# The last pair of the first network: down product by seven products of halves, with weight sums made in the same pair

## The chip, the core and the metric

The kernel runs on one core of a Trainium2 chip. The core has TensorE (PE, matmuls into PSUM), VectorE (DVE), ScalarE (ACT), GpSimd (POOL) and SyncE (SP). Each has an instruction queue of its own that runs in order. SP and ACT issue the DMAs of this kernel, and 16 DMA engines carry them. The metric is the device time in microseconds (us), the median of several executions; one more execution was recorded by the hardware profiler.

## The reference

All data are float32. Attention in chunks of 64 tokens gives x (4608 x 512); then come two networks, each with an up product, a gate, and a down product.

```python
x = ...                                        # attention, 4608 x 512
xn = x / sqrt(mean(x * x) + 1e-6) * rms_g
g, val = xn @ w_gate, xn @ w_val               # 512 -> 1536 each
y = (g * sigmoid(g) * val) @ w_out             # 1536 -> 512, the first network
h = y @ w_in2                                  # 512 -> 2048
out = (h * clip(h + 3, 0, 6) / 6) @ w_out2     # 2048 -> 512, the second network
```

The inputs of attention are drawn as normal numbers of a spread near 0.38 for q and k and 0.1 for v.

## The kernel before

A matrix is kept as two parts of reduced float32 (F32R), a high one and the rest, and a product takes three matmuls: high by high, low weight by high, high weight by low. Tokens go in nine blocks of 512. Blocks 0 to 2 of the first network are computed plainly; blocks 3 to 8 go in three pairs (the loop over `p`, L1359).

In a pair, the up matrix works by seven products of halves in place of eight (`Operands` makes the sums of the weights once, early, and keeps them in DRAM as `ops`; `x_ops` makes those of the inputs). There are 84 products of six matmuls each (`product`), in groups of 14: in a group the products 1, 1, 4, 3, 4, 3, 5, 6, 5, 6, 2, 7, 2, 7 follow each other, numbered by the table at L1394 on, each with a half `m` of 128 columns. Products 1 and 2 gather in PSUM banks 2 and 3 of this pair (`bank(0, m)`), 4, 6 and 7 in banks 6 and 7, 3 and 5 in banks 4 and 5. Behind each product ACT copies or applies silu out of PSUM, VectorE adds or multiplies out of PSUM (L1357), POOL multiplies the two branches. The activations are left in tiles `ge` (one big one) and `gu`.

The down matrix of the pair is computed plainly (`mm_down_a`): 24 items, one for each of 12 slices of 128 rows and each of the two blocks, 12 matmuls an item. `split_wp` makes the two parts of an activation (ACT the high one, POOL the rest), two items ahead. The weights `w_out` in two parts were kept in DRAM as `keep_out` by `keep_w`.

What sets the order is written out by hand. `Loads` (L456) has a list of all weight tiles in the order of use; each tile used up issues the next load on SP's queue, six tiles ahead of use; a load's tile comes from a pool of 36 buffers. A `tick` (L1194) stands behind every second up product and every down item; a pair has 66 ticks. At a tick the functions run that `at(t, ...)` put there: units of attention (in the first two pairs alone), the second network's weights (`Stash`: raw weights loaded by ACT's queue, turned on ACT, VectorE and POOL, and stored to `stash_in` and `stash_out` in 24 ticks each, eight times, until the end of this pair), norms, and the sums of inputs. In the last pair's down half SP also loads block 0 of y (`load_x2`), fourteen of the second network's down weights (`fetch_out`) and the first six tiles of its stream (`Stream`, in the attention's buffers q, k, qT, kT, p, v).

The second network's pairs do their down product by seven products of halves already: `product_down` (L1578), 56 steps of six matmuls; `feed` splits an activation four steps ahead, on VectorE. Its weight sums were made by `turn_out` during the second network's block 0.

The lines that the prediction speaks of:

```python
def product(bank, op, x, first=True, last=True): ...   # six matmuls, L1029
yb = [(*bk[0], *bk[1]), (*bk[4], *bk[0])]               # L1452, down items
t = gt(f0, 0)
vec(t, t, bank(0, 1), ALU.mult)                         # product 2, half 1: empties bank 0's second half
```

## Time and profile before

| | |
|---|---|
| median of 3 runs | 1655.03 us (1654.75 to 1655.18) |
| the profiled execution | 1654.2 us |
| its span in the trace | 1652.4 us |
| TensorE busy | 1640.0 us, 99% |
| VectorE, ACT, POOL busy | 1030.2, 846.1, 453.4 us (62%, 51%, 27%) |
| moved by DMA | 375.08 MB, mean 227 GB/s |

The span begins with the first instruction of the program and ends with the last; the profiled execution's time has 1.8 us around it. Times inside the trace are counted from the span's start. An engine that is busy for less of the span isn't therefore without effect: TensorE waits for it wherever it is late with one instruction.

### The profile page before, as it was taken

The numbers are of one execution on the slowest core, as the hardware profiler recorded it, in microseconds if no ns is written. First come the engines' busy times: TensorE is split into PE (matmuls) and PEld (weight loads), VectorE is DVE, ScalarE is ACT, GpSimd is POOL, SyncE is SP. The second block draws the span as 40 slices with busy tenths as digits, with TensorE's granted clock in tenths as the row PEclk, the third lists the DMA queues.
The fourth block names the chain that finished last, engine by engine and source line by source line (L and its number), as shares of the span: only waits on it lengthen the run. The fifth ranks groups of instructions, "written<-read, shape, count | busy, mean of one in ns | idle before, by whom it ended". The sixth has DMA issues, their size and how long they took to land.

```text
span 1652.4 us, 26451 instructions
## 1 busy us (share of the span) xinstructions
PE 1640.0 (99%) x9920; PEld 1350.1 (82%) x9920; DVE 1030.2 (62%) x1533; ACT 846.1 (51%) x1409; POOL 453.4 (27%) x333
## 2 busy tenths in 40 slices
PE   8999999999999999999999999999999999999999
PEld 7788887888888888888888888888888888888887
DVE  6887566655575755748334388358746764875475
ACT  6885445355464454635444334455545544654553
POOL 1002434322226432354226522141024003301310
PEclk8999999999999999999999999999999999999999
DMA  9914776738976688865979676767876796788666
GB/s 303 277 44 100 212 208 204 224 135 248 314 263 226 208 286 289 274 210 199 346 241 327 260 268 205 228 192 249 219 216 219 214 243 197 224 222 231 196 194 163
DMA packets 336098, 375.08 MB, mean 227 GB/s; under 512 B 184289, under 2 KB 260065, under 8 KB 335841
## 3 DMA queue, kind: packets, MB, share of 16 engines
q1 hardware_dynamic: 266080, 302.32, 59.7%
q10 hardware_dynamic: 69888, 71.06, 12.6%
q8 instruction: 79, 1.29, 0.3%
q14 instruction: 51, 0.41, 0.1%
HBM read 292.55 MB, written 80.74 MB: 226 GB/s over the span
## 4 chain that ended last, share of the span: by engine, by line
PE 95%; DVE 2%; DMA 1%; ACT 1%; issue 0%; SPq 0%; POOL 0%; DVEq 0%; POOLq 0%
PE PS L1029 39%; PE PS L1581 18%; PE PS L1018 13%; PE PS L1043 6%; PE PS L1044 6%; PE PS L1046 6%; PE PS L923 1%; PE PS L850 1%; DMA wo<-ops 1%; PE PS L832 1%; PE PS L1051 1%; PE PS L1055 1%; PE PS L1052 1%; PE PS L1783 1%; PE PS L794 0%
## 5 line engine op out<-in xcount | busy, mean ns | idle before, releaser
L1029 PE MATMUL PS<-xu,wo 128*128 128x512 f32 x1512 | 350.2, 391 | 0.5 <-DVE xu L1243 0.5
L1029 PEld LDWEIGHTS PS<-xu,wo 128*128 128x128 f32 x1512 | 282.1, 188 | 59.8 <-DVE xu L1243 0.9
L1029 PE MATMUL PS<-xo,wq 128*128 128x512 f32 x1344 | 305.3, 389 | 0.0
L1581 PE MATMUL PS<-gs,wq 128*128 128x512 f32 x1296 | 295.3, 389 | 0.0
L1029 PEld LDWEIGHTS PS<-xo,wq 128*128 128x128 f32 x1344 | 252.3, 188 | 52.4
L1581 PEld LDWEIGHTS PS<-gs,wq 128*128 128x128 f32 x1296 | 242.9, 188 | 51.7 <-DVE gs L1575 1.2
L1018 PE MATMUL PS<-XH,w 128*128 128x512 f32 x576 | 147.9, 399 | 2.7 <-ACT XH L656 1.9
L1018 PEld LDWEIGHTS PS<-XH,w 128*128 128x128 f32 x576 | 107.1, 190 | 26.4 <-ACT XH L656 2.2
L1043 PE MATMUL PS<-gs,wd 128*128 128x512 f32 x288 | 113.2, 393 | 0.0
L1044 PE MATMUL PS<-gs,wd 128*128 128x512 f32 x288 | 112.2, 389 | 0.0
L1074 POOL TENSOR_TENSOR al<-sg,ah 128x512 fp32r<-128x512 f32 x40 | 55.8, 1396 | 154.6 <-ACT ah L1072 150.3
L1353 POOL TENSOR_TENSOR gs<-gu,gs 128x512 fp32r<-128x512 f32 x60 | 84.3, 1423 | 45.9 <-ACT gs L1352 39.9
L1357 DVE TENSOR_TENSOR gu<-gu,PS 128x512 f32<-128x512 f32 x60 | 41.1, 686 | 83.0 <-ACT gu L1439 45.8
L1649 POOL TENSOR_TENSOR gt<-gx 128x512 f32<-128x512 f32 x8 | 10.3, 1290 | 296.5 <-DVE gx L1646 296.5
L1575 DVE TENSOR_TENSOR gs<-gu,gs 128x512 fp32r<-128x512 f32 x88 | 67.9, 791 | 32.0 <-ACT gs L1574 31.7
L1574 ACT CAST gs<-gt 128x512 fp32r<-128x512 f32 x96 | 58.1, 623 | 43.9 <-DVE gt L1718 33.5
L1512 DVE SCALAR_TENSOR_TENSOR gu<-gu,PS 128x512 f32<-128x512 f32 x48 | 32.8, 684 | 72.9 <-ACT gu L1509 72.9
L1018 PE MATMUL PS<-XL,w 128*128 128x512 f32 x288 | 77.9, 393 | 0.0
L1046 PE MATMUL PS<-gs,wd 128*128 128x512 f32 x288 | 77.0, 389 | 0.0
L1072 ACT CAST ah<-sg 128x512 fp32r<-128x512 f32 x52 | 32.4, 624 | 84.7 <-DVE sg L1330 53.2
L1574 ACT CAST gs<-gu 128x512 fp32r<-128x512 f32 x96 | 57.4, 621 | 25.2 <-DVE gs L1575 17.7
L1649 POOL TENSOR_TENSOR gt<-gu 128x512 f32<-128x512 f32 x24 | 32.5, 1355 | 129.0 <-DVE gu L1646 124.9
(249 smaller groups left out, 2823.8 us busy)
## 6 DMA issues: line engine op xcount, KB each, us to landing
wq<-stash_in SPq DMA_DIRECT2D x128, 512.0 KB
wo<-ops SPq DMA_DIRECT2D x126, 512.0 KB
wq<-sums_out SPq DMA_DIRECT2D x64, 512.0 KB
wq<-stash_out SPq DMA_DIRECT2D x48, 512.0 KB
wd<-keep_out SPq DMA_DIRECT2D x36, 512.0 KB
yd<-yst SPq DMA_DIRECT2D x18, 512.0 KB
ops<-w ACTq DMA_DIRECT2D x36, 256.0 KB
v<-in_v_dram SPq DMA_DIRECT2D x32, 256.0 KB
```

What stands on the lines that cost most here:

```text
L1018: nc.tensor.matmul(ps, w(wi, c), xs[c][xi], start=(i == 0), stop=(i == n - 1))
L1029: nc.tensor.matmul(PS[:, bank, :], op[:, wi, c * 128:(c + 1) * 128], x[xi][:, c, :], start=first and i == 0, stop=last and i == 5, skip_gr ...
L1043: nc.tensor.matmul(ps, wm[0], a[0], start=first, stop=False)
L1044: nc.tensor.matmul(ps, wm[1], a[0], start=False, stop=False)
L1046: nc.tensor.matmul(PS[:, banks[m], :], w[:, 0, m * 128:(m + 1) * 128], a[1], start=False, stop=last)
L1074: nc.gpsimd.tensor_tensor(lo, t, hi.bitcast(F32), op=ALU.subtract)
L1353: e.tensor_tensor(w[:, 1, :], t, w[:, 0, :].bitcast(F32), op=ALU.subtract)
L1357: nc.vector.tensor_tensor(o, x, y, op=op)
L1574: nc.scalar.copy(w[:, 0, :], x)
L1575: e.tensor_tensor(w[:, 1, :], x, w[:, 0, :].bitcast(F32), op=ALU.subtract)
L1581: nc.tensor.matmul(PS[:, banks[m], :], op[:, wi, m * 128:(m + 1) * 128], x[xi], start=first and (wi, xi) == (0, 0), stop=False, skip_group ...
L1649: nc.gpsimd.tensor_tensor(slot(i, "t"), slot(i, "12"), slot(i, "11"), op=ALU.subtract)
```

## The change

For the last pair alone the 24 down items become 42 steps of `product_down`: seven products for each of six pairs of slices, the activations of both blocks combined, and the output columns in two halves.

- The sums of weights that four of the seven products need are made by a new class `OutSums`, six rounds, one for each pair of slices, from three ticks before the pair begins, one every four ticks. A round loads two kept weights (`load`, on SP's queue, into the attention's buffers q and k), adds their two parts (`whole`, two ticks later, VectorE), makes four sums (`sums`, one tick on, VectorE), splits them (`split`, one tick on, ACT and VectorE) and stores them to `keep_sums` (`keep`, one tick on, four DMAs on ACT's queue).
- `Loads` fetches 21 tiles for this pair's down product in place of 12: nine from `keep_sums`, twelve by halves from `keep_out` (two DMAs each).
- Activations lie in other tiles (`slot`: XL, the attention's v, q, k, and the pool); two POOL subtractions a group (`sums_g`) begin the combined activations. VectorE ends them (12 subtractions) and splits them in `feed`, four steps ahead; the first four splits are POOL's, in the last up group.
- Results leave PSUM by `kept` (two ACT copies) and `more` (two VectorE additions of bank 4 and 5) and are stored by `y_put`.
- Eight of the fetches of the second network's down weights stay in this half; eight are issued in the next stage, whose PSUM banks change places.

```diff
@@ -450,6 +450,56 @@
+    e1 = dr_p.tile([128, 4, NI, 2, 256], F32, name="keep_sums")
...
+    class OutSums:
+        def buf(self, tag, kind=F32):
+            return at_p.tile([128, 2, 512], kind, tag=tag, name="os")
+
+        def load(self):
+            self.r = [self.buf(tag) for tag in ("q", "k")]
+            for z in range(2):
+                nc.sync.dma_start(out=self.r[z], in_=o1[2 * self.i + z])
+
+        def whole(self):
+            self.u = self.buf("qT")
+            for z in range(2):
+                nc.vector.tensor_tensor(self.u[:, z, :], self.r[z][:, 0, :], self.r[z][:, 1, :], op=ALU.add)
+
+        def sums(self):
+            (a11, a21), (a12, a22) = ((self.u[:, z, 0:256], self.u[:, z, 256:512]) for z in range(2))
+            tt = nc.vector.tensor_tensor
+            tt(a22, a21, a22, op=ALU.add)
+            tt(a21, a11, a21, op=ALU.subtract)
+            tt(a11, a22, a11, op=ALU.subtract)
+            tt(a12, a12, a11, op=ALU.subtract)
+
+        def split(self, z):
+            if z == 0:
+                self.w = [self.buf(tag, F32R) for tag in ("kT", "p")]
+            w, u = self.w[z], self.u[:, z, :]
+            nc.scalar.copy(w[:, 0, :], u)
+            nc.vector.tensor_tensor(w[:, 1, :], u, w[:, 0, :].bitcast(F32), op=ALU.subtract)
+
+        def keep(self):
+            for z in range(2):
+                for y in range(2):
+                    nc.scalar.dma_start(
+                        out=e1[:, 2 * z:2 * z + 2, self.i, y, :],
+                        in_=self.w[z].bitcast(F32)[:, y, :].rearrange("p (k n) -> p k n", k=2),
+                    )
+
+        def plan(self, t0):
+            for d, fn, *args in (
+                (0, self.load), (2, self.whole), (3, self.sums), (4, self.split, 0), (4, self.split, 1), (5, self.keep)
+            ):
+                at(t0 + d, fn, *args, turn=3)
+
...
@@ -468,6 +518,16 @@
+                elif p_ == 2:
+                    t = wp.tile([128, 2, 2, 256], F32R, tag="w", name="wd")
+                    if k_ < 4:
+                        nc.sync.dma_start(out=t.bitcast(F32), in_=e1[:, k_, 2 * i:2 * i + 2])
+                    else:
+                        z, h = divmod(k_ - 4, 2)
+                        for n in range(2):
+                            nc.sync.dma_start(
+                                out=t.bitcast(F32)[:, n], in_=o1[4 * i + z + 2 * n][:, :, h * 256:(h + 1) * 256]
+                            )
                 else:
                     t = wp.tile([128, 2, 512], F32R, tag="w", name="wd")
                     nc.sync.dma_start(out=t.bitcast(F32), in_=o1[i])
@@ -1226,7 +1286,13 @@
-            order += [(p, "out", f, 0) for f in range(FA)]
+            if p < 2:
+                order += [(p, "out", f, 0) for f in range(FA)]
+        O2, O3, O4, O1, O11, O21, O12, O22 = range(8)
+        for k_, part in ((O11, 3), (O1, 3), (O2, 3), (O12, 2), (O3, 3), (O12, -1), (O4, 3), (O22, 3)):
+            order += [(2, "out", j, k_) for j in (range(part) if part > 0 else range(3 + part, 3))]
+        for i in range(NI):
+            OutSums(i).plan(P0 + 2 * PAIR - 3 + 4 * i)
         loads = Loads(order)
...
@@ -1361,7 +1444,26 @@
+            def slot(i, name):
+                key = ("t", i // 2) if name == "t" else ("1", i // 2 if i < 2 else i) if name[0] == "1" else ("2", i)
+                if key not in g:
+                    if key[0] == "1" and i < 2:
+                        g[key] = xn_p.tile([128, KD, N], F32, tag="XL", name="ge")
+                    elif key[0] == "1" and i > 2:
+                        g[key] = at_p.tile([128, 2, N], F32, tag=("v", "q", "k")[i - 3], name="ga")
+                    else:
+                        g[key] = wp.tile([128, 2, N], F32, tag="w", name="gu")
+                n = i % 2 if name == "t" else int(name[1]) - 1 + (2 * i if name[0] == "1" and i < 2 else 0)
+                return g[key][:, n, :]
+
+            def sums_g(i):
+                nc.gpsimd.tensor_tensor(slot(i, "t"), slot(i, "12"), slot(i, "11"), op=ALU.subtract)
+                x = slot(i, "12")
+                nc.gpsimd.tensor_tensor(x, slot(i, "22"), x, op=ALU.subtract)
+
             def gt(f, z):
+                if p == 2:
+                    return slot(f // 2, "%d%d" % (f % 2 + 1, z + 1))
...
@@ -1401,6 +1504,8 @@
+                    if p == 2 and i == NI - 1 and pr in (2, 7):
+                        nx.append(split_by(nc.gpsimd, slot(len(nx), "11")))
...
+                        if p == 2:
+                            sums_g(i_)
...
@@ -1445,30 +1552,95 @@
-                    if i == NI and n > 1:
+                    if p < 2 and i == NI and n > 1:
...
-            yb = [(*bk[0], *bk[1]), (*bk[4], *bk[0])]
...
+            if p < 2:
+                yb = [(*bk[0], *bk[1]), (*bk[4], *bk[0])]
...
+            steps = [
+                (pr, i)
+                for pr, span in (
+                    (1, range(NI)), (5, range(NI)), (6, range(NI)), (2, range(4)), (7, range(NI)),
+                    (2, range(4, NI)), (3, range(NI)), (4, range(NI)),
+                )
+                for i in span
+            ]
+
+            def feed(n):
+                if n + 2 < len(steps) and steps[n + 2][0] in (6, 4):
+                    pr, i = steps[n + 2]
+                    t = slot(i, "t")
+                    vec(t, slot(i, "22" if pr == 6 else "21"), t, ALU.subtract)
+                if n < len(steps):
+                    pr, i = steps[n]
+                    x = slot(i, {1: "11", 5: "t", 6: "t", 2: "21", 7: "12", 3: "22", 4: "t"}[pr])
+                    nx.append(split_by(nc.vector, x))
+            def kept(pool, z):
...
+            def more(t):
...
+            for n, (pr, i) in enumerate(steps):
+                k_, z = {
+                    1: (O11, 0), 2: (O12, 0), 3: (O4, 4), 4: (O22, 1), 5: (O1, 4), 6: (O2, 1), 7: (O3, 1),
+                }[pr]
+                key = (p, "out", i // 2, k_)
+                product_down(bk[z], loads.t[key][:, i % 2], nx.popleft(), pr in (1, 5) and i == 0)
+                if i % 2 == 1:
+                    loads.t.pop(key)
                     loads.ahead(1)
-                if p == 2:
-                    if n == 12:
+                if i == NI - 1:
+                    if pr == 1:
+                        for m in range(2):
+                            copy(bank(1, m), bank(0, m))
+                    elif pr == 6:
+                        u2 = kept(wp, 1)
+                    elif pr == 7:
+                        c = kept(st_p, 1)
+                        more(c)
+                        y_put(c, b + 1, 1)
+                    elif pr == 2:
+                        y_put(kept(st_p, 0), b, 0)
+                    elif pr == 3:
+                        more(u2)
+                        y_put(u2, b + 1, 0)
+                    elif pr == 4:
+                        y_put(kept(st_p, 1), b, 1)
+                feed(n + 4)
+                j = n * 24 // 42
+                if (n + 1) * 24 // 42 == j:
+                    continue
+                if j == 12:
+                    load_x2(0)
+                    XS = [xn_p.tile([128, KD, N], F32R, tag=tag, name="xr") for tag in ("XH", "XL")]
+                    xs[:] = [(XS[0][:, c, :], XS[1][:, c, :]) for c in range(KD)]
+                elif j == 18:
+                    x2 = xf.pop(0)
+                    x_split([x2[:, c, :] for c in range(KD)])
+                    stream.ahead(6)
+                if 13 < j < 22:
+                    stash[(j - 14) // 2].fetch_out(j % 2)
                 tick()
@@ -1517,7 +1689,7 @@
-            bank = 6 + n % 2
+            bank = 2 + n % 2
...
-            if n == 4:
-                for z in range(2):
-                    stash[NQ - 1].fetch_out(z)
+            if n < 8:
+                stash[4 + n // 2].fetch_out(n % 2)
```

How this stands on the queues. First SP in the up half of the last pair, before: loads of operands (`wo`, 512 KB each) alone.

```order
L467 DMA wo_8197<-ops2_121 128x1024
L467 DMA wo_8224<-ops3_122 128x1024
L467 DMA wo_8235<-ops2_121 128x1024
L467 DMA wo_8266<-ops2_121 128x1024
L467 DMA wo_8274<-ops3_122 128x1024
L467 DMA wo_8308<-ops3_122 128x1024
```

And after, around the fifth round's two loads (`os`, 512 KB each):

```order
L517 DMA wo_8240<-ops2_121 128x1024
L517 DMA wo_8250<-ops2_121 128x1024
L517 DMA wo_8271<-ops2_121 128x1024
L467 DMA os_8300<-keep_out8_133 128x1024
L467 DMA os_8301<-keep_out9_134 128x1024
L517 DMA wo_8312<-ops3_122 128x1024
L517 DMA wo_8323<-ops2_121 128x1024
```

The loads of the sums stand between the operand loads, after 13 operand loads of this pair (`wo` behind the first six), and what follows on SP is behind them. They wait until `whole` of the fourth round has read the same buffers.

Next VectorE in the third group of the up half, before: additions and multiplications out of PSUM (L1357) and pieces of `Stash` (L255, L256, L259). The last row is the multiplication that empties bank 0's second half.

```order
L1357 TENSOR_TENSOR gu_8118<-gu_8118,PS_103 128x512
L1357 TENSOR_TENSOR ge_8007<-ge_8007,PS_103 128x512
L1357 TENSOR_TENSOR s2_8140<-s2_8140,PS_103 128x512
L255 TENSOR_SCALAR sc_8239<-sc_8239 128x512
L256 TENSOR_SCALAR sc_8239<-sc_8239 128x512
L259 SCALAR_TENSOR_TENSOR sraw_8104<-sraw_8104,sc_8239 128x512
L255 TENSOR_SCALAR sc_8281<-sc_8281 128x512
L256 TENSOR_SCALAR sc_8281<-sc_8281 128x512
L1357 TENSOR_TENSOR gu_8257<-gu_8257,PS_103 128x512
L259 SCALAR_TENSOR_TENSOR sraw_8216<-sraw_8216,sc_8281 128x512
L1357 TENSOR_TENSOR gu_8291<-gu_8291,PS_103 128x512
```

And after, from the second addition of the fifth round's `whole` (`os_8353`) to the last row ahead of the same multiplication (here `gu_8351`, which comes next):

```order
L472 TENSOR_TENSOR os_8353<-os_8301 128x512
L259 SCALAR_TENSOR_TENSOR sraw_8157<-sraw_8157,sc_8333 128x512
L477 TENSOR_TENSOR os_8353<-os_8353 128x256
L478 TENSOR_TENSOR os_8353<-os_8353 128x256
L479 TENSOR_TENSOR os_8353<-os_8353 128x256
L480 TENSOR_TENSOR os_8353<-os_8353 128x256
L255 TENSOR_SCALAR sc_8382<-sc_8382 128x512
L256 TENSOR_SCALAR sc_8382<-sc_8382 128x512
L1440 TENSOR_TENSOR gu_8399<-gu_8399,PS_103 128x512
L487 TENSOR_TENSOR os_8402<-os_8353,os_8402 128x512
L487 TENSOR_TENSOR os_8403<-os_8353,os_8403 128x512
L259 SCALAR_TENSOR_TENSOR sraw_8304<-sraw_8304,sc_8382 128x512
```

Twelve rows run there between the arrival of the loads and the multiplication, seven of them of the sums; the stash pieces and the addition out of PSUM (L1440, before L1357) stood there before. The change moves no instruction of the other queues in this place but ACT's two casts and four stores a round.

## Rows read from the trace of the kernel before

**Rows 1.** The page: busy time of TensorE, and the chain by engine.
```profile
PE 1640.0 (99%) x9920; PEld 1350.1 (82%) x9920; DVE 1030.2 (62%) x1533; ACT 846.1 (51%) x1409; POOL 453.4 (27%) x333
...
PE 95%; DVE 2%; DMA 1%; ACT 1%; issue 0%; SPq 0%; POOL 0%; DVEq 0%; POOLq 0%
```

**Rows 2.** TensorE's waits, the longest: us in total, times, longest.
```profile
PE PS L1018 <- ACT XH L656: 1.9, 1, 1.9
```

**Rows 3.** Timeline of TensorE where stages begin: start, us, line, tiles, count.
```profile
769.89 12.40 PE L1029 MATMUL PS<-xu,wo 128*128 128x512 f32 x54
...
884.13 0.39 PE L1043 MATMUL PS<-gs,wd 128*128 128x512 f32 x1
...
949.41 1.98 PE L1018 MATMUL PS<-xr,wq 128*128 128x512 f32 x8
```

**Rows 4.** Windows: us, busy of PE, PEld, DVE, ACT, POOL; clock, DMA share, GB/s.
```profile
755.00:770.00 15.00, 15.00 (x68) 12.43 (x67) 14.90 (x18) 5.20 (x9) 8.35 (x6) 1.00 0.12 43
...
774.00:803.00 29.00, 29.00 (x130) 24.02 (x129) 13.86 (x23) 15.38 (x25) 8.33 (x6) 1.00 0.99 351
...
832.00:836.00 4.00, 4.00 (x19) 3.34 (x18) 1.55 (x3) 1.72 (x3) 0.12 (x1) 1.00 1.03 421
...
884.00:949.00 65.00, 65.00 (x289) 53.83 (x288) 24.15 (x21) 21.15 (x39) 44.40 (x32) 1.00 0.80 299
...
1113.00:1189.00 76.00, 76.00 (x336) 62.59 (x335) 65.81 (x100) 43.21 (x76) 6.22 (x4) 1.00 0.80 238
```

**Rows 5.** DMAs that ACT issues from 772 to 808: count, KB each.
```profile
sraw<-in_moe_w_out_dram ACTq DMA_DIRECT2D x2, 512.0 KB
stash_in<-slo ACTq DMA_DIRECT2D x3, 256.0 KB
stash_in<-shi ACTq DMA_DIRECT2D x2, 256.0 KB
sraw<-in_moe_w_in_dram ACTq DMA_DIRECT2D x1, 512.0 KB
stash_in<-sc ACTq DMA_DIRECT2D x1, 256.0 KB
stash_out<-sc ACTq DMA_DIRECT2D x1, 256.0 KB
stash_out<-slo ACTq DMA_DIRECT2D x1, 256.0 KB
```

**Rows 6.** Timeline of VectorE: the multiplication that empties bank 0's second half, third group.
```profile
820.87 0.68 DVE L1357 TENSOR_TENSOR gu<-gu,PS 128x512 f32<-128x512 f32 x1
```

**Rows 7.** VectorE by line, 770 to 884: count, busy, mean ns; idle before.
```profile
L1357 DVE TENSOR_TENSOR gu<-gu,PS 128x512 f32<-128x512 f32 x19 | 13.0, 686 | 34.8 <-ACT gu L1439 22.7 <-PE PS L1029 9.7 <-ACT gu L1348 2.2
...
L256 DVE TENSOR_SCALAR sc<-sc 128x512 uint32<-128x512 uint32 x8 | 5.4, 670 | 0.3
L259 DVE SCALAR_TENSOR_TENSOR sraw<-sraw,sc 128x512 uint32<-128x512 uint32 x7 | 4.8, 690 | 0.1
L255 DVE TENSOR_SCALAR sc<-sc 128x512 f32<-128x512 f32 x8 | 4.6, 571 | 10.6 <-ACT sc L139 10.6
```

**Rows 8.** VectorE by line, 985 to 1036: the second network's weight sums.
```profile
L390 DVE TENSOR_TENSOR oh<-ou,oh 128x512 fp32r<-128x512 f32 x10 | 9.8, 1023 | 6.0 <-ACT oh L389 6.0
...
L378 DVE TENSOR_TENSOR ou<-w 128x512 f32<-128x512 f32 x10 | 6.4, 683 | 0.0
...
L384 DVE TENSOR_TENSOR ou<-ou 128x256 f32<-128x256 f32 x5 | 2.1, 425 | 0.2
```

**Rows 9.** VectorE by line, 1113 to 1189: a split in the second network's down half.
```profile
L1575 DVE TENSOR_TENSOR gs<-gt,gs 128x512 fp32r<-128x512 f32 x24 | 16.0, 683 | 0.0
```

**Rows 10.** VectorE and ACT by line, 884 to 949.
```profile
L259 DVE SCALAR_TENSOR_TENSOR sraw<-sraw,sc 128x512 uint32<-128x512 uint32 x4 | 5.7, 1419 | 0.1
...
L1082 ACT COPY yst<-PS 128x512 f32<-128x512 f32 x3 | 1.7, 589 | 20.1 <-PE PS L1046 20.1
```

**Rows 11.** SP's waits, 770 to 884: us in total, times, longest.
```profile
SPq L467 <- DMA stash_in<-slo: 15.6, 2, 8.3
```

More of the change, by code (lines that the diff above doesn't have):

```diff
@@ L1306, in fused_kernel @@
         A11, S2_, S1_, S3_, A12, S4_, A21, A22 = range(8)
-        O2, O3, O4, O1, O11, O21, O12, O22 = range(8)
         NG = NQ // 2
@@ L1354, in split_wp, with split_by, product_down @@
             return w[:, 0, :], w[:, 1, :]
+        def split_by(e, x):
+            w = wp.tile([128, 2, N], F32R, tag="w", name="gs")
+            nc.scalar.copy(w[:, 0, :], x)
+            e.tensor_tensor(w[:, 1, :], x, w[:, 0, :].bitcast(F32), op=ALU.subtract)
+            return w[:, 0, :], w[:, 1, :]
+        def product_down(banks, op, x, first):
+            for wi, xi in ((0, 0), (1, 0), (0, 1)):
+                for m in range(2):
+                    nc.tensor.matmul(
+                        PS[:, banks[m], :],
+                        op[:, wi, m * 128:(m + 1) * 128],
+                        x[xi],
+                        start=first and (wi, xi) == (0, 0),
+                        stop=False,
+                        skip_group_check=True,
+                    )
         def vec(o, x, y, op):
@@ new lines, in kept, with y_put @@
+            def kept(pool, z):
+                t = pool.tile([128, 2, N], F32, tag="w" if pool is wp else "st", name="yc")
+                for m in range(2):
+                    copy(t[:, m, :], bank(z, m))
+                return t
+            def more(t):
+                for m in range(2):
+                    vec(t[:, m, :], t[:, m, :], bank(4, m), ALU.add)
+            def y_put(t, blk, h):
+                nc.sync.dma_start(out=yd[blk][:, 2 * h:2 * h + 2, :], in_=t)
+            for n, (pr, i) in enumerate(steps):
[6 more added lines that the diff above has]
+                    loads.t.pop(key)
+                    loads.ahead(1)
+                if i == NI - 1:
+                    if pr == 1:
+                        for m in range(2):
+                            copy(bank(1, m), bank(0, m))
[15 more added lines that the diff above has]
+                if (n + 1) * 24 // 42 == j:
+                    continue
+                if j == 12:
[8 more added lines that the diff above has]
+                    stash[(j - 14) // 2].fetch_out(j % 2)
```

55 lines of the change are left out of this document (18 added, 37 removed).

## Prediction

> **What bounds the kernel now.** I read the page's busy times and its chain first: TensorE is busy 99% of the span, and 95% of the chain that ended last is TensorE itself [rows 1]. Then the list of TensorE's waits: the longest is 1.9 us in all, far ahead of the stretch that the change touches [rows 2]. So the kernel is bound by the number of matmuls, and an edit elsewhere matters only where it makes TensorE wait. The timeline of TensorE dates the stretch. The last pair's up products begin at 769.89, its down products at 884.13, the second network at 949.41 [rows 3]. The 288 down matmuls of the pair thus take 65.28 us, or 0.2267 us each (the 389 ns that rows of single matmuls show are overlapped ends). The up part has 84 products of six matmuls in 114.24 us: 1.360 us a product, 2.72 us a tick of two products. Last I read the DMA share by windows: it is 0.12 at 755 to 770, and 0.99 at 774 to 803 [rows 4]. There the DMA engines are full already before anything is added, and TensorE doesn't wait only because its loads are issued early.
>
> **The gain.** 42 steps of 6 matmuls replace 24 items of 12: 252 for 288. 36 x 0.2267 = 8.2 us less on TensorE, on the path in full if nothing else becomes late.
>
> **The engines in the down half.** Splits go from POOL to VectorE. In 42 x 1.360 = 57.1 us VectorE gets 38 splits and 12 subtractions for the "t" sums at 0.683 [rows 9], 4 additions from PSUM at 0.686 [rows 7], three stash pieces at 0.571 + 0.670 + 0.690 = 1.93 [rows 7], four stash sums at 0.425 [rows 8] and two x splits at 0.683: 34.2 + 2.7 + 5.8 + 1.7 + 1.4 = 45.8 us, 80% of the stretch. The second network's down half runs the same steps with the same lead of four at 65.81 of 76 us (87%) without a TensorE wait [rows 4]. So I take nothing for it. The other bound: where POOL works beside it, VectorE's instructions are longer, a split 1.023 [rows 8] and the last stash instruction 1.419 [rows 10]. That makes 38 x 0.34 + 3 x 0.73 = 15.1 us more, 60.9 in all, 3.8 over the stretch; the lead of four products (5.4 us) hides that unless it is used up elsewhere. POOL itself was busy 44.40 of 65 us here [rows 4] and loses its splits. One wait is new: after product 7 ends, two ACT copies (0.589 each [rows 10]) and the second addition (0.686) must be through before product 3 writes bank 4, two steps (2.72 us) later: 1.9 us, with 0.8 to spare. For a late ACT I count 0.2. A gain I exclude, since no wait of TensorE is there to go.
>
> **DMA in the down half and behind it.** Weight loads rise from 5 left to 15 left in this stretch, out2 fetches fall from 14 to 8: 10 x 0.524 - 6 x 0.524 and one y store more make 2.6 MB on top of 299 GB/s x 65 us = 19.4 MB [rows 4], so 22.0 MB. Of these, four streamed tiles and four fetches (4.2 MB) may land in the next stage: 17.8 MB in 57.1 us needs 312 GB/s, and 351 are to be had [rows 4]. I take nothing; if all had to land, 22.0 / 0.351 = 62.7 us would be 5.6 us too long. The eight fetches that move behind 949 are wanted eight steps later. The swapped PSUM banks, and products kept in XL and the attention's buffers, add no instruction: nothing.
>
> **The sums in the up half: the term that decides.** Six rounds, one every 4 ticks (10.9 us), each read two weights (2 x 524 KB on SP's queue), and run on VectorE two additions, four half-width sums and two splits. Three ticks on, ACT issues four stores of 262 KB. VectorE's work is about 4.4 us a round (2 x 0.683, 4 x 0.425 [rows 8], 2 x 0.683) and fits by itself. The bytes do not. 2.1 MB a round are 193 GB/s on top of DMA engines that are full at 351 GB/s. The first round's loads fall into the idle stretch before 770; the other five don't.
>
> What it costs is read from the place where VectorE waits. `whole` stands in VectorE's order two ticks behind its load, and everything behind it waits with it, the reads of PSUM among them. The worst is the fifth round. Ahead of its loads in the program stand, from 774.0: 2 y stores, 13 operand loads and 8 loads of sums, its own included (23 x 0.524 = 12.06 MB); 12 stores of sums (3.15 MB); and from ACT 3 raw loads and 8 stash stores, issued up to 808 [rows 5] (1.57 + 2.10 MB). Together 18.9 MB. Before the change, SP's loads waited on ACT's older transfers again and again [rows 11], so I let the two queues advance in the program's order. The rate has two ends in the rows: 351 GB/s held over 29 us, and 421 over 4 us of loads alone [rows 4]. I take their middle, 386, since neither mix is that of the new stretch. 18.9 / 0.386 = 48.9 us, so the loads land at 822.9.
>
> Behind that on VectorE come: the second addition 0.68, the end of a stash piece 0.69, four sums 1.70, the next piece 1.24, one addition from PSUM 0.69, two splits 1.37, a stash instruction 0.69, and then the multiplication that empties bank 0's second half, 0.69 [rows 7 to 9]. That is 7.7 us: 830.6. Before the change that multiplication starts at 820.87 [rows 6], and the next product that writes this bank is number 39 of the pair, at 769.89 + 39 x 1.360 = 822.9. So TensorE waits **7.7 us**. The ends: at 421 GB/s 3.6 us, at 351 GB/s 12.6 us. The sixth round by the same count (four operand loads, two loads and four stores of sums more: 23.1 MB, 833.8, then two VectorE instructions, 1.4 us, for product 44 at 829.7) is 5.5 us late, which the first wait covers. The operand loads behind it have six ticks' lead and are late by less. No gain here.
>
> The trace shows 421 GB/s for 4 us and no more than 351 over a long full stretch [rows 4]. The Trainium skill, "DMA: Bandwidth & Descriptors" (Specifications), gives a limit of about 358 GB/s for one core's HBM traffic; the short stretch is above it, the long one agrees. By 358 the loads would land at 826.7 and the wait be 11.5 us, and that speaks against this change; it is the third case below.
>
> **Sum.** -8.2 + 7.7 + 0.2 = -0.3 us. The profiled execution took 1654.2 us (span 1652.4 and 1.8 around it) and gives 1653.9; it is 0.8 under the runs' median of 1655.03, so in medians 1654.7. About 0.2% (3.3 us) is what a measurement of this kernel can tell from no change, and so I forecast no measurable difference.
>
> **Rivals.** *There is room.* SP can issue loads earlier than their place, as it does now, and the landing leads of the operands are used up instead of TensorE's time. For it: 0.12 of share before 770, and 421 GB/s [rows 4]. Against: the loads of sums stand behind operand loads in one queue and are wanted earlier. At 421 GB/s 3.6 us go back, 1650.6; with full room -8.2, 1646.9. *The DMA engines give no more than 351.* For it: the only long full stretch [rows 4]. TensorE then waits 12.6 us at product 39: -8.2 + 12.6 + 0.2 = +4.6, 1659.7, **slower**; the change gains and loses alike where the loads land at 823.2, at 384 GB/s, and a slowdown that can be measured begins near 360. *VectorE is the bound in the down half as well.* If the waits above have used up the lead, the 3.8 us come on top: 1658.5. For it: the longer instructions beside POOL; against it: 87% without a wait in the second network.
>
> **How the numbers follow.** Forecast 0.45 (its own range 1651 to 1658.5), room 0.25, full engines 0.20, VectorE 0.07, something unseen 0.03. Faster by over 0.2% (below 1651.7): room 0.25 and 0.09 of the forecast's low end, 0.34. Within 0.2%: 0.33 of the forecast and 0.02 of the VectorE case, 0.35. Slower: the rest, 0.31. The range that leaves out 2 in 10 reaches from 1647.5 (all but the very best of the case with room) to 1661 (full engines and a little more).
>
> **What would show it.** Right: TensorE's waits list a line of VectorE (the multiplication or addition from PSUM) or of ACT between 800 and 835 with 4 to 11 us in all; the DMA share is 0.95 or more from 774 to about 835; VectorE's `whole` waits for the loads of sums by several us in rounds three to six; the down half has 252 matmuls at 0.227 us and no wait over 1 us. Wrong: no TensorE wait in the up half (then the time is near 1647), or waits for operand loads or in the down half, or a DMA share under 0.9 beside late sums, which would make it a matter of order on the queues and not of bytes.

## The result, and the profile after

The changed kernel takes 1669.72 us (median of 4 runs, 1668.79 to 1670.46) where the kernel before took 1654.89 (1653.78 to 1655.18) beside it: ratio 1.0093, 95% interval 1.008 to 1.0105. It is slower by 14.8 us, and outside the range forecast. The profiled execution took 1670.46 us, its span 1668.4.

The pair begins at 771.31 us instead of 769.89. In the profiles of this study the pair begins between 769.4 and 773.3 us, although the kernels don't differ ahead of about 760; so stages are compared, not spans:

| stage, us | before | after | difference |
|---|---|---|---|
| up half of the last pair | 114.24 | 127.22 | +13.0 |
| its down half | 65.28 | 59.92 | -5.4 |
| block 0 of the second network | 87.42 | 94.03 | +6.6 |
| the rest | 615.59 | 615.91 | +0.3 |

The differences add up to 14.5 us, close to the 14.8 of the medians. The page's busy times after, for [rows 1]; TensorE runs 36 matmuls less and is busy as long, part of it at half its clock:

```profile
PE 1640.4 (98%) x9884; PEld 1345.0 (81%) x9884; DVE 1088.1 (65%) x1630; ACT 865.0 (52%) x1445; POOL 448.9 (27%) x326
```

TensorE's waits after (us in total, times, longest), from 772 to 1060, a stretch in which the kernel before had none:

```profile
PE PS L1111 <- ACT ah L1132: 4.8, 1, 4.8
PE PS L1089 <- DVE gu L1440: 2.9, 1, 2.9
PE PS L1089 <- DVE ge L1440: 2.1, 2, 1.7
PE PS L1430 <- DVE gs L1424: 1.7, 2, 0.9
PE PS L1089 <- ACT ge L1413: 1.5, 1, 1.5
PE PS L1089 <- DVE xu L1309: 1.1, 1, 1.1
PE PS L1089 <- ACT PS L1526: 0.9, 1, 0.9
```

L1089 is the up products, L1430 the down products, L1111 block 0. The up half has not one wait but six, of 8.5 us in all, and VectorE and ACT take turns as the one waited for. The windows of after, in the columns of [rows 4]:

```profile
774.00:803.00 29.00, 24.69 (x103) 18.50 (x101) 25.15 (x42) 12.25 (x22) 4.81 (x3) 1.00 1.01 376
803.00:835.00 32.00, 28.22 (x121) 22.21 (x120) 22.97 (x35) 16.72 (x30) 13.61 (x10) 1.00 1.04 384
774.00:835.00 61.00, 52.91 (x223) 40.72 (x221) 48.12 (x77) 28.97 (x51) 18.41 (x13) 1.00 1.03 380
836.80:840.20 3.40, 3.40 (x10) 2.62 (x10) 1.81 (x2) 0.25 (x1) 0.75 (x1) 0.53 1.02 336
...
977.00:983.80 6.80, 4.05 (x10) 3.18 (x11) 6.66 (x10) 1.83 (x3) 1.62 (x1) 0.50 0.93 369
```

In the first row TensorE falls from 29.00 to 24.69 us, and VectorE rises from 13.86 to 25.15 of 29. The DMA engines are full, at 380 GB/s over 61 us. Twice the granted clock is at its lower level, 1.2 GHz. In the up half that is for 3.4 us, and TensorE had waited 2.9 us and then worked 1.4 us when it fell. In block 0 it is for 6.8 us: it falls when TensorE has stood for 2 us of its 4.8, so TensorE works in only 4.05 of these 6.8 us.

VectorE's waits for the sums' loads, in the same columns as TensorE's, from 774 to 850:

```profile
DVE os L472 <- DMA os<-keep_out: 2.3, 2, 1.4
```

That is all there is of the wait on which the forecast rested. In the fifth round, which it named, there is none: VectorE's timeline has no idle time ahead of the two additions.

```profile
827.00 1.28 DVE L472 TENSOR_TENSOR os<-os 128x512 f32<-128x512 f32 x2
```

By the trace's semaphores the two loads had landed at 822.6 and 823.9, close to the 822.9 of the forecast. The wait of 2.9 us ends at 835.58, with 234 matmuls or 39 products of the pair done, so it is the very place that the forecast named; but VectorE came late to it for other reasons than the loads.

ACT's timeline (start, us, engine, line) shows a wait that the forecast didn't have:

```profile
791.27 0.37 ACTq L290 DMA_DIRECT2D stash_in<-shi  x1
791.73 0.83 ACTq L290 DMA_DIRECT2D stash_in<-slo  x1
...
796.07 1.14 ACT L486 CAST os<-os 128x512 fp32r<-128x512 f32 x2 [3.76 <-DMA os<-keep_out]
797.12 0.59 ACT L1413 ACTIVATE gu<-PS 128x512 f32<-128x512 f32 x1
797.74 0.57 ACT L1517 COPY PS<-PS 128x512 f32<-128x512 f32 x1
797.75 5.01 ACTq L492 DMA_DIRECT2D keep_sums<-os  x4
802.80 0.63 ACT L1413 ACTIVATE ge<-ge 128x512 f32<-128x512 f32 x1 [4.49 <-DMA keep_sums<-os]
...
803.34 0.58 ACT L1526 COPY PS<-PS 128x512 f32<-128x512 f32 x1
```

ACT idles 3.76 us ahead of the round's copy (L486). The row names a load, but what the copy reads is VectorE's sum, and the third of VectorE's four sums (L479) ended at 796.05, just before it: here ACT waited for VectorE. Then its four stores (L492) take 5.01 us to issue. By the trace's semaphores the third was held until 799.30 and the fourth until 802.32, when the two stash stores at the top of the rows landed, 8.0 and 10.6 us after their issue. The activation behind them in ACT's queue idles 4.49 us. The copy out of PSUM after it (L1526) ends at 803.92, and with it TensorE's wait of 0.9 us.

In block 0 the place to look is SP's queue, first after and then before (same columns):

```profile
959.89 0.65 SPq L337 DMA_DIRECT2D w<-stash_out  x1
963.63 1.09 SPq L363 DMA_DIRECT2D wq<-stash_in  x2
965.56 0.32 SPq L337 DMA_DIRECT2D w<-stash_out  x1
966.85 0.53 SPq L1656 DMA_DIRECT2D x<-yd  x1
968.36 0.52 SPq L1657 DMA_DIRECT2D x<-yd  x1
```

```profile
955.53 0.57 SPq L1484 DMA_DIRECT2D x<-yd  x1
956.14 0.61 SPq L1485 DMA_DIRECT2D x<-yd  x1
```

The x tiles for the next blocks are issued 11 to 12 us later. Block 0 itself begins 9.0 us later (958.45 instead of 949.41), so counted from its start they are 2.3 and 3.2 us late. They also take longer to arrive, 8.7 us from the second issue to VectorE's start instead of 6.7. VectorE stops for them, with block 0's gates behind it (VectorE's timeline, first after and then before):

```profile
977.03 0.69 DVE L1664 TENSOR_TENSOR xt<-x 128x512 f32<-128x512 f32 x1 [6.46 <-DMA x<-yd]
```

```profile
962.86 0.69 DVE L1492 TENSOR_TENSOR xt<-x 128x512 f32<-128x512 f32 x1 [1.33 <-issue]
```

That is 18.58 us into block 0 in place of 13.45: 5.1 us late, near TensorE's wait of 4.8.

### The profile page after: what moved, and what is told of

Same layout as the page of the kernel before. It is cut to its first block, busy times and chain, and to the rows that moved or that the text cites. A ratio compares the mean times of both kernels' runs of the same rounds, so it can differ in the third digit from the quotient of the medians.

```text
span 1668.4 us, 26650 instructions
## 1 busy us (share of the span) xinstructions
PE 1640.4 (98%) x9884; PEld 1345.0 (81%) x9884; DVE 1088.1 (65%) x1630; ACT 865.0 (52%) x1445; POOL 448.9 (27%) x326
## 4 chain that ended last, share of the span: by engine, by line
PE 47%; DVE 2%; DMA 1%; issue 1%; ACT 0%; ACTq 0%; DVEq 0%; SPq 0%
PE PS L1089 22%; PE PS L1430 20%; PE PS L1078 2%; PE PS L1111 1%; PE PS L1112 1%; PE PS L1115 1%; PE PS L1936 1%; DVE gs L1424 1%; DMA stash_out<-slo 1%; DMA sums_out<-oh 0%; DVE gu L1440 0%; DMA wd<-keep_sums 0%; DVE os L472 0%; DVE os L487 0%; DVE xr L1069 0%
## 5 line engine op out<-in xcount | busy, mean ns | idle before, releaser
L1089 PE MATMUL PS<-xu,wo 128*128 128x512 f32 x1512 | 354.7, 393 | 9.2 <-DVE gu L1440 2.9
L1089 PEld LDWEIGHTS PS<-xu,wo 128*128 128x128 f32 x1512 | 282.3, 189 | 72.7 <-DVE gu L1440 3.6
L1089 PE MATMUL PS<-xo,wq 128*128 128x512 f32 x1344 | 305.3, 389 | 0.0
L1430 PE MATMUL PS<-gs,wq 128*128 128x512 f32 x1296 | 295.3, 389 | 0.0
L1089 PEld LDWEIGHTS PS<-xo,wq 128*128 128x128 f32 x1344 | 252.3, 188 | 52.3
L1430 PEld LDWEIGHTS PS<-gs,wq 128*128 128x128 f32 x1296 | 242.9, 188 | 51.8 <-DVE gs L1424 1.2
L1424 DVE TENSOR_TENSOR gs<-gu,gs 128x512 fp32r<-128x512 f32 x119 | 93.9, 810 | 32.9 <-ACT gs L1423 32.5
L1423 ACT CAST gs<-gu 128x512 fp32r<-128x512 f32 x128 | 76.3, 621 | 38.3 <-DVE gs L1424 17.7
L1440 DVE TENSOR_TENSOR gu<-gu,PS 128x512 f32<-128x512 f32 x54 | 36.9, 686 | 67.4 <-ACT gu L1546 36.3
L1103 PE MATMUL PS<-gs,wd 128*128 128x512 f32 x192 | 75.9, 395 | 0.0
L1104 PE MATMUL PS<-gs,wd 128*128 128x512 f32 x192 | 74.8, 390 | 0.0
L272 POOL TENSOR_TENSOR slo<-sraw,sc 128x512 fp32r<-128x512 f32 x32 | 48.4, 1513 | 81.0 <-ACT sc L271 64.7
L1799 DVE SCALAR_TENSOR_TENSOR gu<-r,gu 128x512 f32<-128x512 f32 x48 | 42.3, 880 | 36.4 <-ACT r L1681 36.0
```

Source lines behind the costliest of these rows:

```text
L272: nc.gpsimd.tensor_tensor(lo, x, hi.bitcast(F32), op=ALU.subtract)
L1089: nc.tensor.matmul(PS[:, bank, :], op[:, wi, c * 128:(c + 1) * 128], x[xi][:, c, :], start=first and i == 0, stop=last and i == 5, skip_gr ...
L1103: nc.tensor.matmul(ps, wm[0], a[0], start=first, stop=False)
L1104: nc.tensor.matmul(ps, wm[1], a[0], start=False, stop=False)
L1423: nc.scalar.copy(w[:, 0, :], x)
L1424: e.tensor_tensor(w[:, 1, :], x, w[:, 0, :].bitcast(F32), op=ALU.subtract)
```

## The experiments

Each was timed beside the kernel before. Stages are of the one profiled execution; before has 114.24, 65.28 and 87.42. In all runs but one, what the three stages gain or lose together is within 1.5 us of what the medians say, so a small difference of one stage wants the medians beside it. The exception is e4 (3.1 us), whose profiled execution was the slowest of its four.

| run | up | down | block 0 | median | ratio (95%) |
|---|---|---|---|---|---|
| after | 127.22 | 59.92 | 94.03 | 1669.72 | 1.0093 (1.008 to 1.0105) |
| e1_no_sums | 114.24 | 59.43 | 93.95 | 1657.22 | 1.0013 (1.0003 to 1.0022) |
| e2_no_stores | 121.27 | 59.44 | 94.35 | 1664.46 | 1.0055 (1.0039 to 1.007) |
| e3_no_loads | 125.36 | 60.01 | 96.05 | 1668.75 | 1.0081 (1.0063 to 1.0099) |
| e4_fetch_later | 127.02 | 60.15 | 92.36 | 1664.64 | 1.0055 (1.0038 to 1.0072) |
| e5_work_only | 120.35 | 59.40 | 95.06 | 1664.16 | 1.0052 (1.0037 to 1.0066) |
| e6_rounds_later | 124.79 | 59.39 | 93.22 | 1664.62 | 1.0057 (1.0038 to 1.0077) |
| e7_on_pool | 137.39 | 59.43 | 93.57 | 1677.87 | 1.0135 (1.0112 to 1.0158) |
| e8_x_first | 126.91 | 60.22 | 87.23 | 1661.77 | 1.004 (1.0026 to 1.0053) |
| e9_sp_stores | 126.65 | 59.43 | 87.04 | 1661.77 | 1.0041 (1.0026 to 1.0056) |
| e10_spread | 126.84 | 59.43 | 87.04 | 1661.92 | 1.0046 (1.0031 to 1.0061) |
| e11_spread_sp | 121.97 | 59.39 | 87.04 | 1655.81 | 1.0005 (0.9996 to 1.0015) |
| e12_two_buffers | 115.44 | 59.97 | 87.45 | 1651.85 | 0.9975 (0.9966 to 0.9984) |
| e13_two_buffers_act | 117.95 | 59.39 | 87.04 | 1652.05 | 0.9977 (0.9968 to 0.9986) |
| e14_spread_work_only | 114.63 | 59.39 | 87.04 | 1650.78 | 0.9971 (0.9959 to 0.9982) |
| e15_x_split_earlier | 115.83 | 57.67 | 88.73 | 1650.79 | 0.9969 (0.9958 to 0.998) |

**Which part of the change loses time: e1 to e4.**

e1 takes the rounds out:

```diff
-        for i in range(NI):
-            OutSums(i).plan(P0 + 2 * PAIR - 3 + 4 * i)
```

> Left out: the six rounds of weight sums; the nine tiles of sums are fetched from kept operands of the same size and packet length, so that the down half moves the same bytes. Up half after: 127.2 us, 13.0 over the 114.2 of before. If the rounds cause all of that (every theory of the up half), it is back at 114.2 to 115. The theory that the later losses are of their own (the down half 2.8 us over its 57.1, block 0 of the second network 6.6 us over 87.4) expects these to stay: 1655 - 8.2 + 2.8 + 6.6 = about 1656. The rival, that the later losses are only a backlog that the up half hands on, expects them to go too: about 1647.

The up half is back at 114.24 us, so the rounds cost all of the 13.0 us. Block 0 keeps its loss, which is therefore another matter.

e2 leaves out the stores (`(5, self.keep)` in `plan`), e3 the loads (`(0, self.load)`).

> Left out: the four stores of each round (24 stores, 6.3 MB, all on ACT's queue); loads, additions and splits stay; the tiles of sums are fetched from kept operands as in the run without sums. Theory 'ACT's stores' (a store waits for older transfers and holds ACT's copies out of PSUM): most of the 13.0 us of the up half goes, 2 or less stays. Theory 'bytes' (the DMA engines are full whoever issues): half of the bytes go, about half of the 13.0 stays or less, 3 to 6 us, as waits for loads. Theory 'VectorE waits for the loads' (that of the prediction): VectorE's additions still stand behind loads, 5 to 8 us stay.

> Left out: the two loads of each round (12 loads, 6.3 MB on SP's queue); the additions read a constant instead, everything behind them stays, the stores too. Theory 'ACT's stores': most of the 13.0 us of the up half stays, 8 or more. Theory 'bytes': about half goes, 3 to 6 us stay. Theory 'VectorE waits for the loads': 2 us or less stay.

Without stores 7.0 us remain, without loads 11.1. The 7.0 lies in the range of the forecast's own theory (5 to 8), but that theory wanted 2 or less without loads. The theory of ACT's stores has its 8 or more without loads, but wanted 2 or less without stores, and the bytes wanted 3 to 6 both times. So none of the three holds by itself. The loads, of which the forecast made the whole cost, are worth 1.9 us of the up half here, and 1.0 by the medians.

e4 issues block 0's eight fetches four steps later:

```diff
-            if n < 8:
-                stash[4 + n // 2].fetch_out(n % 2)
+            if 4 <= n < 12:
+                stash[2 + n // 2].fetch_out(n % 2)
```

> The eight fetches of the second network's down weights that were moved into block 0 are issued from its fifth step on in place of the first; nothing is left out. In the changed kernel VectorE idles 6.5 us there for a load of x that SP issued at 966.9, 11 us later after the stage's start than before. Theory 'the fetches stand ahead of x on SP's queue': the wait of 4.8 us in block 0 and the half clock behind it go, 5 to 6.6 us less: 1663 to 1665. Rival 'the backlog of the down half is what delays x': under 2 us less, 1668 or more.

In the profiled execution block 0 gets 1.7 us back of 6.6, with a wait of 3.4 us left. But that execution took 1669.24 us and the other three 1663.63 to 1665.38; by the medians the edit gives 5.1 us back, as the theory of the fetches said. That the fetches are a cause is shown; whether they are all of it is not. The 11 us of the expectation are differences of trace times; from the stage's start the loads are 2.3 and 3.2 us late.

**Engines, transfers, and the x loads: e5 to e8.** e5 leaves out both loads and stores; e6 moves the rounds (`P0 + 2 * PAIR + 5 + 4 * i`); e7 writes `nc.gpsimd` for `nc.vector` in `whole` and `sums`.

> The six rounds keep only their instructions on VectorE and ScalarE: neither the twelve loads nor the 24 stores are issued (the additions read a constant, and the sum tiles' loads read other stored weights). Theory V (VectorE's own work in its in-order queue is a cause by itself, since VectorE is already full while it prepares the pair's inputs): the up half still takes about 119 to 121 us, near the 121.3 without stores, with waits of TensorE for VectorE near 790 and 830, and the time is about 1662 to 1665. Theory D (only transfers hold the queues, loads and stores each enough alone): the up half is back at 114.2 to 115 and the time is about 1657 to 1658. Block 0 of the second network keeps its 94 us in both.

Theory V held: 6.1 us are lost with no transfer of the rounds. TensorE's waits in e5, from 772 to 900; two of the three (1.7 and 1.1) are the same, to 0.1 us, as in the kernel with loads and stores:

```profile
PE PS L1089 <- DVE ge L1440: 1.7, 1, 1.7
PE PS L1089 <- DVE gu L1440: 1.6, 1, 1.6
PE PS L1089 <- DVE xu L1309: 1.1, 1, 1.1
```

Over 774 to 835, e5's VectorE is busy 55.68 of 61 us:

```profile
774.00:835.00 61.00, 56.53 (x244) 44.88 (x242) 55.68 (x81) 30.72 (x54) 22.34 (x15) 1.00 0.86 298
```

And VectorE's timeline of e5 ahead of the wait for `xu` (L1309, an input of the pair that TensorE waits for until 792.1):

```profile
785.95 0.68 DVE L1309 TENSOR_TENSOR xu<-xf,xu 128x512 fp32r<-128x512 f32 x1
786.55 2.42 DVE L472 TENSOR_TENSOR os<-ones 128x512 f32<-128x512 f32 x2
788.89 0.68 DVE L1440 TENSOR_TENSOR gu<-gu,PS 128x512 f32<-128x512 f32 x1
790.80 0.69 DVE L1440 TENSOR_TENSOR s<-s,PS 128x512 f32<-128x512 f32 x1 [1.23 <-issue]
791.40 0.68 DVE L1309 TENSOR_TENSOR xu<-xf,xu 128x512 fp32r<-128x512 f32 x1
```

The second round's two additions, 2.42 us for what the forecast counted as 1.37, stand between two input splits. In the kernel after, with the loaded weights, they take 1.83 and 0.68 us at this place.

> All six rounds start eight ticks (about 22 us) later, behind the stretch in which VectorE prepares the pair's inputs; bytes, instructions and spacing stay. Theory V: the waits near 785 to 800 go and others stay away, since VectorE has about 37% of its time in use there and the rounds add about 50%: the up half loses 3 to 6 us instead of 13.0, time about 1660 to 1663. Theory D: the rounds' loads and stores still meet DMA engines that are full until 835, and the first round no longer has the idle stretch before 770: the up half loses 10 to 14 us as now or more, and the time is 1667 to 1671.

The waits of 785 to 800 went, as theory V said, but 10.6 us were lost all the same, at new places from 810 on. Neither theory alone is enough, and the time, 1664.62, lies between their ranges.

> The two additions and four half-width sums of each round run on GpSimd instead of VectorE (about 4.2 of the 5.5 us that a round takes on VectorE now); the two splits, all loads and all stores stay. Theory V: TensorE's waits for VectorE become small and those for ScalarE, which the stores hold, remain: the up half loses 5 to 9 us instead of 13.0, time about 1662 to 1666. Theory D: nothing is gained, 13 us, 1668 to 1671; it could be more, as GpSimd is slower at it and keeps come later.

Wrong for both: 23.2 us lost. VectorE falls to 28.94 of 61 us, but an addition takes 1.399 us on POOL, and the copies on ACT, which wait for them, hold ACT's queue: TensorE waits 8.2 us for ACT's L1413.

e8 loads the first x tile at the end of the down half:

```diff
+                if j == 21:
+                    x_first = x4_load(1, 0)
...
-        fill = x_fill(1)
+        fill = x_fill(1, x_first)
```

> The first two loads of x for block 0 of the second network are issued at the end of the down half, ahead of the last two stores of the pair's output on SyncE's queue, instead of behind them and eight fetches. If block 0's loss is these late loads alone, block 0 goes from 94.0 back to 87.5 to 89 and the time from 1669.7 to about 1663 to 1665. Rival: the queue's bytes are the limit, and the second pair of x loads or a fetch comes late in their place: block 0 takes 91 to 94, time 1667 to 1670. The up half keeps its 127 us.

Block 0 is back at 87.23 us, all of the loss; its wait of 4.8 us is gone. That late x loads are the cause is shown; how much of their lateness comes from the fetches, and how much from the other transfers ahead of them, is not. From 900 to 1060 e8 has these waits of TensorE only:

```profile
PE PS L1436 <- DVE gs L1430: 0.9, 1, 0.9
PE PS L1436 <- DMA stash_out<-slo: 0.7, 1, 0.7
```

**The two causes one by one and together: e9 to e11, all on e8.** e9 has `nc.sync.dma_start` for `nc.scalar.dma_start` in `keep`; e10 spreads the rounds and moves them seven ticks; e11 does both.

```diff
-                (0, self.load), (2, self.whole), (3, self.sums), (4, self.split, 0), (4, self.split, 1), (5, self.keep)
+                (0, self.load), (2, self.whole, 0), (3, self.whole, 1), (3, self.sums, 0), (4, self.sums, 1, 2),
+                (5, self.sums, 3), (5, self.split, 0), (6, self.split, 1), (6, self.keep, 0), (7, self.keep, 1),
```

> As the kernel with the early x loads (e8), and the 24 stores of the rounds are issued by SyncE instead of ScalarE; bytes and order stay. Theory: ScalarE's own queue, held by stores that wait for older transfers, is the part of the up half's 12.7 us that the stores bring (about 5 to 6 us; VectorE's work 6.1 and the loads 1 remain): up half 120.5 to 122.5, time 1655.5 to 1657.5. Rival: the stores cost by their bytes in full DMA engines, whoever issues them, or they hold SyncE's operand loads instead: up half 125 to 129, time 1660 to 1664.

> As e8, and the rounds begin seven ticks (19 us) later, behind VectorE's preparation of the pair's inputs, with their instructions spread over six ticks in pieces of at most 1.6 us of VectorE a tick (the stores follow each split); bytes, instructions and ScalarE's stores stay. Theory: VectorE's bursts in its in-order queue cost 6.1 us of the up half; spread out they cost 0 to 2, and the stores' part of 5 to 6 us stays: up half 120 to 122.5, time 1655 to 1657.5. Rival: it is VectorE's whole load or the full DMA engines, so that the waits only move, as they did when the rounds were moved without being spread (10.6 us): up half 123 to 126, time 1658 to 1661.

> Both edits together on e8: rounds later and spread, their stores issued by SyncE. If the two causes are separate and both undone by this, the up half loses 0 to 3 us: 114.5 to 117.5, time 1649.5 to 1652.5, below the kernel before (1654.9). Rival: full DMA engines (380 GB/s for 61 us) put a floor under it, late operand loads then show as TensorE's or VectorE's waits: up half 119 to 124, time 1654 to 1659.

e9 and e10 missed: each gave at most 0.3 us (12.4 and 12.6 us lost, 12.7 in e8). Together they gave 4.9, and 7.7 us stayed, which is the range of the rival, a floor by full DMA engines. But in e11 ACT's largest wait, from 774 to 890, was its round's copy, held until the one buffer of the halves had been stored:

```profile
ACT os L488 <- DMA keep_sums<-os: 12.0, 6, 3.2
```

In e10, where ACT issued the stores, the same copies waited 11.9 us.

**Two buffers: e12 to e14.** e12 is e11 with a second set of buffers (`st` and `XH`, free in this half) for odd rounds, the subtraction a tick behind its copy, a round every five ticks, and the loads seven to ten ticks ahead of use in place of two:

```diff
+            if self.i % 2 == 0:
+                self.r = [self.buf(tag) for tag in ("q", "k")]
+            else:
+                self.r = [st_p.tile([128, 2, 512], F32, tag="st", name="os") for _ in range(2)]
...
+                (0, self.whole, 0), (1, self.whole, 1), (1, self.sums, 0), (2, self.sums, 1, 2, 3), (2, self.high, 0),
+                (3, self.low, 0), (3, self.high, 1), (4, self.low, 1), (5, self.keep, 0), (6, self.keep, 1),
...
+            OutSums(i).plan(P0 + 2 * PAIR + (-3, 4, 10, 15, 20, 25)[i], P0 + 2 * PAIR + (7, 12, 17, 22, 27, 32)[i])
```

> As e11 (early x loads, rounds later and spread, stores by SyncE), and besides: two sets of buffers for the loads and for the halves that are stored, a tick between ScalarE's copy and VectorE's subtraction, and one round every five ticks. Theory B (what is left in e11, 7.7 us of the up half, is engines held by copies that wait until the one buffer is stored, 12.0 us of ScalarE's waits there): up half 114.5 to 117.5, time 1648 to 1651.5, faster than the kernel before. Theory D (a floor by bytes: about 45.7 MB want through 114 us at 380 to 385 GB/s): up half 118.5 to 122, time 1652 to 1656, with waits on operand loads.

Theory B held: 1.2 us lost, and the kernel is faster than before, by 0.25% (0.16 to 0.34). TensorE's waits in e12 from 772 to 1060, and its windows:

```profile
PE PS L1446 <- DVE gs L1440: 1.7, 2, 0.9
PE PS L1099 <- ACT gu L1562: 0.4, 1, 0.4
PE PS L1099 <- DVE gu L1456: 0.2, 1, 0.2
```

```profile
774.00:803.00 29.00, 29.00 (x130) 24.01 (x129) 21.07 (x30) 15.26 (x27) 10.52 (x7) 1.00 0.99 366
803.00:835.00 32.00, 31.80 (x140) 26.00 (x139) 27.60 (x37) 15.02 (x27) 13.03 (x10) 1.00 1.03 372
835.00:887.10 52.10, 51.73 (x228) 42.50 (x227) 37.61 (x53) 25.51 (x46) 27.71 (x19) 1.00 1.04 382
```

The DMA engines are as full as in the slow kernel (0.99 to 1.04), now to the end of the half, VectorE is busy 86.28 of 113.1 us, and TensorE loses next to nothing. Full DMA engines by themselves cost little here: e14, below, puts the transfers at about 1 us.

> As e12 with the 24 stores back on ScalarE. If ScalarE held by its stores is a cause once VectorE's work is spread: up half 3 to 6 us longer than e12's. If the one set of buffers was what made the stores matter: within 1 us of e12.

2.5 us more than e12 in the profiled up half, between the two expectations, and medians that can't be told apart (1652.05, 1651.85): with two buffers and this spacing it matters little who issues the stores.

> As e12 without the rounds' loads and stores (the additions read a constant, the sum tiles' loads read other stored weights): VectorE's and ScalarE's work alone, spread and late. If the 6.1 us that this work cost alone in its first place came from its place beside the preparation of the inputs and from bursts: up half 114.2 to 115.2, time 1647 to 1648.5. If it is the amount: 117 to 120, time 1650 to 1653. What e12 takes above this is the transfers' part.

0.4 us lost: the work that cost 6.1 us in its first place costs almost nothing spread and later. Above it, e12's transfers cost 0.8 us of the up half, and 1.1 by the medians. The time missed its range of 1647 to 1648.5, since the down half keeps the 2.3 us that it takes over 57.1.

**The down half: e15.** The second network's x is loaded and split earlier (`j == 9` and `j == 14` for 12 and 18).

> As e12, and the second network's first x tile is fetched three and split four of the 24 places earlier in the down half, before the subtractions for product 4 come on VectorE. Theory: the down half's 2.3 to 2.9 us above 57.1 (two waits on VectorE's splits, while VectorE and GpSimd split x side by side and a split takes 1.78 us instead of 0.68) are this meeting: down half 57.1 to 57.8, time about 2 us below e12's, 1649 to 1650.5. Rival: VectorE is at its limit in the whole down half (about 80% by the count of the prediction), and the wait only moves: down half 59 to 60, time 1651 to 1653.

The down half falls to 57.67 us, as the theory said; block 0 takes 1.3 us more, with a wait of 0.6 for ACT. What stood there in e12, VectorE's timeline and then POOL's:

```profile
936.08 1.78 DVE L1440 TENSOR_TENSOR gs<-gu,gs 128x512 fp32r<-128x512 f32 x1
937.79 2.37 DVE L1079 TENSOR_TENSOR xr<-xf,xr 128x512 fp32r<-128x512 f32 x2
```

```profile
935.52 3.48 POOL L1079 TENSOR_TENSOR xr<-xf,xr 128x512 fp32r<-128x512 f32 x2 [2.93 <-ACT xr L1077]
```

A split takes 1.78 us there instead of 0.683, with POOL at work from 935.52 on, right ahead of product 4, whose inputs each need a subtraction and a split. TensorE's two waits in e12's down half (1.7 us) stand in that product, and e15 has neither. e15 is 0.9969 of before (0.9958 to 0.998) and can't be told from e12.

## Why the prediction was wrong, point by point

The forecast was 0.3 us less, and the stages came to 14.5 us more. Of the 14.8 between them the up half has 5.3 (13.0 instead of 7.7), block 0 has 6.6 (instead of nothing), and the down half 2.8; the rest is 0.3, and the 0.2 that the forecast had for a late ACT in the down half didn't come. The up half's 7.7 was, besides, put down to the wrong wait.

- **The gain of 8.2 us** is there: 252 matmuls at 0.2267 us are 57.1, and e15 comes to 57.67. The changed kernel got 5.4 of it. The step that failed by 2.8 us is "the lead of four products (5.4 us) hides that": the 60.9 us for VectorE beside POOL were spread evenly in the count, but they fall together where x is split (e15).
- **"I take nothing"**, for the DMAs in the down half and behind it, failed by 6.6 us in block 0. I asked when the eight fetches are wanted, not what stands behind them on SP's queue: the x loads, and on VectorE block 0's gates behind x. Issuing the x loads earlier gave all of it back (e8).
- **"VectorE's work is about 4.4 us a round ... and fits by itself"** failed by 6.1 us (e5). By mean it fits; e14 shows that the amount is not the cause. The first rounds fall on the stretch in which VectorE already prepares the pair's inputs, and in an in-order queue a burst delays what TensorE wants next.
- **The loads' bytes, 7.7 us,** were the wrong term. The rate was right (386 GB/s taken, 380 measured over 61 us), but VectorE waited for the loads 2.3 us in all; leaving them out gave 1.9 us, or 0.9 where the stores are gone too (e2 against e5). Where the loads land (822.9 forecast, 822.6 and 823.9 measured) and the place of the longest wait (product 39) came out right, but VectorE reached the loads only at 827.00, and that wait was 2.9 us and not 7.7. The rival that rested on full DMA engines had 12.6 us for the up half, close to the 13.0 measured; that is luck, since it rested on 351 GB/s and on the same wait for the loads, and it falls with e12. The Trainium skill, "DMA: Bandwidth & Descriptors" (Specifications), has a limit of about 358 GB/s for a core's HBM traffic; the traces don't agree, with 380 GB/s over 61 us after and 382 over 52 in e12. They agree with the Trainium skill, "Perfetto Trace Analysis" (Roofline), by which a core can pull more than that share when it is the only one at work, up to about 435 GB/s.
- **The stores** got bytes in the sum and no wait on ACT. ACT issues them, reads PSUM behind them, and its copies wait for buffers that are being stored. Leaving them out gave 6.0 us (e2), or 5.0 where the loads are gone too (e3 against e5). The issue from ACT's queue is not the whole of it: moved to SP they cost as much (e9), and with e12's buffers and spacing they cost no more on ACT by the medians (e13). This term had no step of its own, and its absence is as large an error as VectorE's.
- **One wait at product 39** was the wrong shape: there were six. Either cause alone keeps TensorE late: undoing one gave at most 0.3 us (e9, e10), both 4.9, and e12's edits besides 6.5 (e11 to e12).
- **The signs** would have misled. From 800 to 836 TensorE waits 4.3 us for VectorE and ACT, the DMA engines are full, and the down half has no wait over 1 us, as "What would show it" asked for a right forecast. Only its third sign, VectorE's waits for the loads, tells the theories apart, and it failed.
- What is not settled: how far e12's 6.5 us belong to the buffers, to the tick between copy and subtraction, to the wider spacing, or to the earlier loads; the four were changed together.

## What to carry to other kernels

Work that "fits" by its mean still has to be placed: read the windows of the engine that gets it, tick by tick, and look at what stands behind each new instruction in each in-order queue, loads and stores too. Where several engines feed one bound engine, undoing one cause at a time can show nothing; take all away first, then put them back one by one. Before new transfers are blamed for their bytes, give them a second buffer, room between the rounds, and a queue on which nothing urgent waits.

## What the runs showed of the hardware that was not expected

- A wait of TensorE costs more than the list says, at the full clock too. In e5 the three waits of the up half come to 4.4 us by the list, and the half is 6.1 us longer with a granted clock of 1.00. Counted from start to start of the matmuls, each of them is 0.16 us longer (the list counts from the end of the matmul before, 0.39 us after its start, where the next one normally starts after 0.2267), and the first matmul behind it takes 0.34 us to the next. The other 0.9 us are hold-ups too short for the list.
- The clock adds to it. In the changed kernel it is at 1.2 GHz for 3.4 us, 1.4 us after a wait of 2.9 (10 matmuls where 15 fit), and for 6.8 us that begin 2 us into a wait of 4.8.
- The DMA engines moved 380 GB/s over 61 us and 382 over 52 with TensorE at work, more than the 351 that the trace before showed over a long stretch [rows 4].
- VectorE's durations depend on what POOL does at the time: 0.683 us and 1.78 us for the same split. In the trace after, no float32 tensor_tensor of 128x512 on VectorE takes over 0.73 us while POOL is idle. Beside POOL the ones that read SBUF alone take up to 2.25 us, and those that read PSUM stay under 0.70.
